# An attention and feed-forward kernel: one batch instead of two ahead of the matrix products, three first tiles in four passes of four chunks

## The chip, the cores and the metric

The kernel runs on one core of a Trainium2 chip. The metric is the device time of one execution in microseconds (us). Three runs of the kernel before took 1062.29, 1059.40 and 1056.72 us, median 1059.4. The execution that was profiled took 1056.42 us by the same clock; its span from the first to the last instruction is 1054.7 us.

The engines are named as in the profile: PE (TensorE, matrix products), PEld (its weight loads), DVE (VectorE), ACT (ScalarE), POOL (GpSimd) and SP (SyncE, which here only issues DMAs).

## The reference

Eight batches, eight heads, 576 positions, 64 numbers per head; then a feed-forward layer over all 4608 tokens with 512 inputs, 2048 inner features and `g = h cos h` between the products.

```python
q_d, k_d, v_d = (a.reshape(B, H, 144, 4, D).mean(axis=3) for a in (q, k, v))
out_d  = softmax(q_d @ k_d.T / 8) @ v_d              # 144 x 144 per head
out_up = np.repeat(out_d, 4, axis=2)
scores = np.where(abs(i - j) < 4, q @ k.T / 8, -1e9)  # a band of 7 keys per query
x = (out_up + softmax(scores) @ v)                   # 576 x 64 per head
x = x.transpose(0, 2, 1, 3).reshape(4608, 512)
h = x @ w_in                                         # w_in 512 x 2048, float64
out = (h * cos(h)) @ w_out                           # w_out 2048 x 512, float64
```

## The kernel before

**Tiles and steps.** The 4608 tokens are cut into 12 tiles of 384 (`NT`), the 2048 features into 16 chunks of 128 (`NC`). A *step* is one chunk of one tile: `gemm1` (L673) makes 12 matmuls (L685) for `h`, ACT and DVE work out `h cos h` (L696 to L704), and two steps later (`LAG`) `gemm2` (L709) adds the chunk's 9 matmuls (L721) into three PSUM banks `po.0` to `po.2`. So a step has 21 matmuls, and there are 192 steps. Both products use a high and a low part of each number (`x0h`, `x0l`, `gh`, `gl`, `wi`, `wo`), which `sub` (L384) makes on POOL or DVE. `PASSES` (L36) is the order of the steps: tiles 0, 1, 2 with chunks 0 to 3, then tiles 0, 1, 2 with chunks 4 to 15, then tiles 3 to 11 with all 16. At the end of a pass the three banks are copied out by ACT (L737) and stored; the first pass of a tile stores through SP (L743), a later pass adds to what is in memory through a DMA that POOL issues (L746). Steps are counted from 0 in this document: tile 1 begins at step 4, chunk 4 is first used at step 12, tile 3 begins at step 48.

**Attention.** A *unit* is one batch and one pair of heads: 32 units of 219 matmuls. `u_qk` (L456) loads q and k and sums groups of four; `u_v` (L481) loads v twice and sums groups of four, on POOL by two additions (L490, L491) or on DVE by one reduction (L492); `u_s` (L496) makes the scores (L513, L521) and the softmax (L534 to L583); `u_t` (L586) transposes (L595, L606); `u_pv` (L612) multiplies by v (L623, L634), adds both parts (L642) and writes the high and low parts of x (L657 to L659). Tile 0 needs batch 0, tile 1 needs batches 0 and 1, tile 2 needs batch 1, tile 3 needs batch 2. x has four slots (`NX`), so tile 4 is written where tile 0 was read. Batches 0 and 1 (`NEARLY`) run ahead of the first step, with PSUM banks that the matrix products use later (`bank`, L444) and with buffers cut from the places of weight chunks 6 to 15 (`ub`, L433). In these early units the row maximum is scaled by a DVE instruction of its own (L557), the exponentials are taken on ACT straight from PSUM (L564), and the last scaling runs on POOL or DVE (L582). Later batches share three banks `pa.0` to `pa.2`.

**Weights.** Weights arrive as float64 words. `w_load` (L389) loads 512 KB; `w_split` (L399) turns it into a high and a low part by an ACT copy (L407), four DVE instructions (L408, L410, L412, L414), an ACT or DVE copy (L418) and a subtraction on POOL or DVE (L386). There are 32 such splits, two per chunk. Their staging buffer is the high half of x slot 3 (L345, L405), and x slot 3 is not written before the last split is through (L364).

**Order.** Nothing runs in the order of the text. `Plan` (L78) collects the operations with their dependencies, costs and due times (`at`, L752), and a list scheduler (L164, L255) lays them out on the engines; each engine then works through its list in that order. Where an operation has alternatives (`alts`), the scheduler picks the engine that would end it earlier. Due times of attention units and weights are given in steps (L759 to L791); those of batch 2 lie between the last step of tile 0, which frees the x slot that tile 4 takes, and the first step of tile 3; `BOOST` (L51) raises the priority of units of batches 0 and 1. All early loads go through one SP queue in the order of `chain` (L804): q and k of batch 0, v of batch 0, q and k of batch 1, weights of chunk 0, v of batch 1, then the other weights. Where PE has a gap in the plan before 300 us, it is filled with matmuls of 128 columns on an identity (L835).

Of the kernel before, what the change touches and what calls it, by code (L numbers as in the profile page):

```python
# [17 lines left out]
ALU = mybir.AluOpType  # L18
# [16 lines left out]
NF = 4  # L35
PASSES = [(t, 0, NF) for t in range(3)] + [(t, NF, NC) for t in range(3)] + [(t, 0, NC) for t in range(3, NT)]  # L36
SD = S // 4
# [12 lines left out]
ON_PE = ()  # L50
BOOST = {0: 100.0, 1: 60.0}  # L51
LAG = 2
# [246 lines left out]
def attn_ffn_kernel(ctx: ExitStack, tc: tile.TileContext, qT, kT, vdn, vl, w_in, w_out, out):  # L299
# [144 lines left out]
    def bank(b, kind):  # L444

        if b < NEARLY:
            tags = {"s": ("pa.0", "po.0", "pa.1", "po.1"), "t": ("ph.0", "ph.1"), "v": ("pa.2", "po.2")}[kind]
            return psum(tags[int(pl.turn("early" + kind, len(tags))[-1])])
        return psum(pl.turn("pa", 3))
# [31 lines left out]
    def u_v(b, pr):  # L481
# [6 lines left out]

        def v_pool():
            pool.tensor_tensor(out=v4()[:, :, 0:2, :], in0=v4()[:, :, 0:2, :], in1=v4()[:, :, 2:4, :], op=ALU.add)  # L490
            pool.tensor_tensor(out=vd.get(), in0=v4()[:, :, 0, :], in1=v4()[:, :, 1, :], op=ALU.add)  # L491
        pl.op("POOL", 2.2, v_pool, w=[vd, vd4], alts=[("DVE", 1.93, lambda: dve.tensor_reduce(  # L492
            out=vd.get(), in_=v4().rearrange("p a r n -> p a n r"), axis=AX.X, op=ALU.add))])
        st[(b, pr)].update(vd=vd, vl=vt)

    def u_s(b, pr):  # L496
# [58 lines left out]
        if early:  # L555

            pl.op("DVE", 0.08, lambda: dve.tensor_scalar(out=mxd.get(), in0=mxd.get(), scalar1=1.0 / 128.0, scalar2=None, op0=ALU.mult),  # L557
                  w=[mxd])

            def exps():  # L560
                act.activation(sml.get(), sml.get(), AF.Exp, scale=0.125)
                for h in range(2):
                    for i in range(2):
                        act.activation(smd.get()[:, h, i], dq(h)[:, i], AF.Exp, bias=mxd.get()[:, h, i:i + 1], scale=1.0 / 128.0,  # L564
                                       accum_out=sud()[:, h, i:i + 1])
            o = pl.op("ACT", _act(n, False) + 4 * (_act(SD, True, 2) + 0.1), exps, r=[mxd, su] + poo, w=[sml, smd], pw=[su2], tab="exp")
            for bk in banks:
# [13 lines left out]
        for sm, part, size, bc in ((sml, sul, n, bl), (smd, sud, m, bd)):  # L581
            f = lambda e, sm=sm, part=part, bc=bc: lambda: e.tensor_tensor(out=sm.get(), in0=sm.get(), in1=bc(part()), op=ALU.mult)  # L582
            pl.op("POOL", _pool(size), f(pool), r=[su], w=[sm], alts=[("DVE", _dve(size), f(dve))])  # L583
        u["sml"], u["smd"] = sml, smd
# [185 lines left out]
    for c in range(NC):  # L770
        for k, d in (("i", 0.0), ("o", 0.7)):
            t = need[c] if c < NF else NF + c - NF
            at(t + d - 4.0, w_load, k, c)
# [3 lines left out]
    for i in range(NPAIR):  # L777
        for t, f in ((-7.9 + 0.5 * i, u_qk), (-4.4 + 0.5 * i, u_v), (-3.4 + i, u_s), (-2.4 + i, u_t), (-1.4 + i, u_pv)):
            at(t, f, 1, i)
# [21 lines left out]
    def ul(f, b):  # L801
        return [(f, b, i) for i in range(NPAIR)]

    chain = [o for k in ul("u_qk", 0) + ul("u_v", 0) + ul("u_qk", 1) + wl(0) + ul("u_v", 1) + wl(*range(1, NC))  # L804
             for o in loads[k]]
    for o, n in zip(chain, chain[1:]):
# [21 lines left out]
    with tc.manual_schedule():  # L828
        constants()
        for o in order:  # L830
            if o.eng == "PE" and o.start < CFG["fend"]:
                s = spare(last, o.start)
                n = int((o.start - s[0] - CFG["fgap"]) / (0.107 if last < 5 else 0.058)) if s else 0
                for _ in range(n):
                    pe.matmul(s[2].get()[:, 0:P], ident_b, ident_b, start=True, stop=True)  # L835
                last = o.start + o.dur
# [36 lines left out]
```

## Time and profile before

| what | value |
|---|---|
| median of three runs | 1059.4 us |
| the profiled execution: time, span | 1056.42 us, 1054.7 us |
| mean granted TensorE clock | 0.974 of full |
| PE busy | 1019.1 us (97%), 11447 matmuls |
| DVE busy | 664.5 us (63%) |
| ACT busy | 619.1 us (59%) |
| POOL busy | 195.8 us (19%) |
| first matmul of step 0 | 87.38 us |

PE is busy nearly all the time after the first fifth, but a busy PE may be a filler or run at half clock, so the share alone tells little of the beginning. The windows below give each engine's busy time per stretch, the number of matmuls in brackets, the granted clock (PEclk, 1.00 is 2.4 GHz and 0.50 is 1.2 GHz) and the share of time in which the 16 DMA engines were busy.

### The profile page before, as it was taken

The page shows a single profiled execution, that of the slowest core. Times are in us where ns is not written, and L with a number is a line of the kernel's source. Part 1 is how long each engine was busy: PE and PEld are TensorE (multiplying, and loading weights), DVE is VectorE, ACT ScalarE, POOL GpSimd, SP SyncE. Part 2 cuts the span into 40 slices and gives each one's busy share as a digit, 9 for nine tenths or more (in the row PEclk, how much of TensorE's full clock was granted, in tenths as well). Part 3 has the DMA queues.
Part 4 walks back from the last instruction along what each step waited for, and adds up shares of the span by engine and source line. Part 5 has one row for each costly group of instructions (what it writes and reads, how often), then busy time and mean ns, then how long its engine had stood idle before and what let it go on. Part 6 is the DMA issues. An engine that isn't in the chain of part 4 may idle for free.

```text
span 1054.7 us, 26617 instructions
## 1 busy us (share of the span) xinstructions
PE 1019.1 (97%) x11447; PEld 899.3 (85%) x11447; DVE 664.5 (63%) x1315; ACT 619.1 (59%) x1194; POOL 195.8 (19%) x239
## 2 busy tenths in 40 slices
PE   6888987999999999999999999999999999999998
PEld 5767876988888898888898888888888888999997
DVE  6686999976548755654636865746546864544442
ACT  2344677766566756655656665646656665655554
POOL 5633445331112310201001310201010300000000
PEclk9577999999999999999999999999999999999999
DMA  9295061031122500300101420301100410000000
GB/s 305 80 346 212 21 215 46 1 55 26 50 57 74 126 31 25 107 24 27 54 27 46 122 63 23 103 18 38 54 27 24 130 54 1 31 1 1 30 1 31
DMA packets 33862, 71.45 MB, mean 68 GB/s; under 512 B 3152, under 2 KB 11344, under 8 KB 33744
## 3 DMA queue, kind: packets, MB, share of 16 engines
q1 hardware_dynamic: 32448, 67.38, 20.0%
q0 software_dynamic: 1296, 2.36, 1.6%
q8 instruction: 90, 1.47, 0.6%
q14 instruction: 28, 0.23, 0.1%
HBM read 57.93 MB, written 11.80 MB: 66 GB/s over the span
## 4 chain that ended last, share of the span: by engine, by line
PE 86%; DVE 8%; issue 3%; ACT 1%; ACTq 0%; POOL 0%; POOLq 0%; DVEq 0%
PE bank L721 34%; PE bank L685 34%; PE bank L634 5%; PE bank L513 3%; PE bank L835 2%; PE bank L623 2%; PE bank L521 2%; DVE xxh L412 2%; PE bank L606 2%; DVE xxh L414 1%; DVE xxh L408 1%; PE bank L595 1%; DVE tr L697 1%; DVE xxh L410 1%; DVE tr L700 1%
## 5 line engine op out<-in xcount | busy, mean ns | idle before, releaser
L721 PE MATMUL bank<-wo,gh 128*128 128x512 f32 x1152 | 365.0, 398 | 0.1
L721 PEld LDWEIGHTS bank<-wo,gh 128*128 128x128 f32 x1152 | 208.8, 188 | 37.4 <-issue 4.0
L721 PE MATMUL bank<-wo,gl 128*128 128x512 f32 x576 | 228.2, 396 | 0.6 <-DVE gl L386 0.5
L700 DVE SCALAR_TENSOR_TENSOR tr<-tr,bank 128x384 f32<-128x384 f32 x192 | 105.8, 551 | 144.1 <-ACT tr L695 144.1
L696 ACT ACTIVATE tr<-bank,bmagic 128x384 f32<-128x384 f32 x192 | 111.3, 580 | 120.2 <-PE bank L685 115.3
L697 DVE SCALAR_TENSOR_TENSOR tr<-tr,bank 128x384 f32<-128x384 f32 x192 | 105.7, 550 | 101.9 <-ACT tr L696 101.5
L694 ACT ACTIVATE tr<-tr 128x384 f32<-128x384 f32 x192 | 100.7, 525 | 84.8 <-DVE tr L697 84.4
L702 ACT ACTIVATE gh<-tr 128x384 fp32r<-128x384 f32 x173 | 90.6, 524 | 95.9 <-DVE tr L700 95.0
L386 DVE TENSOR_TENSOR gl<-tr,gh 128x384 fp32r<-128x384 f32 x163 | 92.9, 570 | 73.2 <-ACT gh L702 72.1
L721 PEld LDWEIGHTS bank<-wo,gl 128*128 128x128 f32 x576 | 108.0, 187 | 25.7 <-DVE gl L386 1.3
L685 PE MATMUL bank<-x0h,wi 128*128 128x384 f32 x384 | 108.6, 344 | 5.7 <-DVE tr L700 5.4
L685 PE MATMUL bank<-x2h,wi 128*128 128x384 f32 x384 | 106.9, 339 | 2.3 <-DVE tr L700 2.3
L685 PE MATMUL bank<-x1h,wi 128*128 128x384 f32 x384 | 106.8, 339 | 1.0 <-DVE tr L700 1.0
L685 PE MATMUL bank<-x3h,wi 128*128 128x384 f32 x384 | 106.9, 339 | 0.1
L695 ACT ACTIVATE tr<-tr 128x384 f32<-128x384 f32 x192 | 100.8, 525 | 6.1
L386 POOL TENSOR_TENSOR gl<-tr,gh 128x384 fp32r<-128x384 f32 x29 | 32.5, 1122 | 313.7 <-DVE gh L703 250.3
L685 PEld LDWEIGHTS bank<-x0h,wi 128*128 128x128 f32 x384 | 71.1, 190 | 9.8 <-DVE tr L700 7.2
L685 PEld LDWEIGHTS bank<-x2h,wi 128*128 128x128 f32 x384 | 70.2, 188 | 5.1 <-DVE tr L700 2.4
L685 PEld LDWEIGHTS bank<-x1h,wi 128*128 128x128 f32 x384 | 70.2, 188 | 4.4 <-DVE tr L700 2.1
L685 PEld LDWEIGHTS bank<-x3h,wi 128*128 128x128 f32 x384 | 70.2, 188 | 2.7 <-issue 0.6
L685 PE MATMUL bank<-x0l,wi 128*128 128x384 f32 x192 | 65.2, 340 | 0.0
L685 PE MATMUL bank<-x3l,wi 128*128 128x384 f32 x192 | 64.5, 336 | 0.0
(188 smaller groups left out, 1501.0 us busy)
## 6 DMA issues: line engine op xcount, KB each, us to landing
vl<-vl SPq DMA_DIRECT2D x26, 384.0 KB
out<-ob SPq DMA_DIRECT2D x36, 256.0 KB
wdi<-w_in SPq DMA_DIRECT2D x16, 512.0 KB
wdo<-w_out SPq DMA_DIRECT2D x16, 512.0 KB
q<-qT SPq DMA_DIRECT2D x26, 292.0 KB
k<-kT SPq DMA_DIRECT2D x26, 292.0 KB
vd<-vdn SPq DMA_DIRECT2D x26, 288.0 KB
out<-ob POOLq DMA_DIRECT2D x9, 256.0 KB, 6.2
```

The source lines that it names most:

```text
L386: f = lambda e: lambda: e.tensor_tensor(out=out(), in0=in0(), in1=in1(), op=ALU.subtract)
L412: pl.op("DVE", 0.7, lambda: dve.scalar_tensor_tensor(out=vi(), in0=wd()[:, :, 1], scalar=-0x40000000, in1=vi(), op0=ALU.bitwise_and, op1=A ...
L513: pe.matmul(banks[h].get()[BS * i:BS * (i + 1), LQ + BS * s:LQ + BS * (s + 1)], q.get()[hs, o:o + BS], k.get()[hs, o:o + BS], start=True, ...
L634: pe.matmul(banks[e].get()[64 * h:64 * h + 64, o:o + BQ], vt.get()[r, a, i, :], ptl.get()[r, a, i, :], start=True, stop=True)
L685: pe.matmul(ph.get()[:, :m], w[:, i, kc, :], x[:, kc, :], start=(n == 0), stop=(n == 3 * KC - 1))
L694: act.activation(tr.get(), tr.get(), AF.Sin, scale=PI)
L695: act.activation(tr.get(), tr.get(), AF.Square)
L696: pl.op("ACT", _act(m, True, 1), lambda: act.activation(tr.get(), h(), AF.Identity, bias=bmagic), r=[ph], w=[tr])
L697: pl.op("DVE", _dve(m), lambda: dve.scalar_tensor_tensor(out=tr.get(), in0=tr.get(), scalar=MAGIC, in1=h(), op0=ALU.subtract, op1=ALU.subt ...
L700: pl.op("DVE", _dve(m), lambda: dve.scalar_tensor_tensor(out=tr.get(), in0=tr.get(), scalar=0.5, in1=h(), op0=ALU.subtract, op1=ALU.mult), ...
L702: pl.op("ACT", _act(m, False), lambda: act.activation(gh.get(), tr.get(), AF.Copy), r=[tr], w=[gh], alts=[("DVE", _dve(m / 2), lambda: dve ...
L721: pe.matmul(o, (gh, gh, gl)[k].get()[:, sl], wo.get()[:, (0, 1, 0)[k]], start=(c == c0 and k == 0), stop=(c == c1 - 1 and k == 2))
```

## The change

- Batch 0 alone keeps the early banks; batch 1 uses the three banks `pa.0` to `pa.2` in turn, has due times from step -4 to step 3.7 instead of -7.9 to 1.6, and half of its former boost (30 for 60).
- `PASSES`: tiles 0, 1, 2 take chunks 0 to 3, then 4 to 7, then 8 to 11, then 12 to 15. Weights of a chunk are due at the step that first uses it: chunks 4 to 7 at step 12, 8 to 11 at step 24, 12 to 15 at step 36 (before, chunk c at step c).
- By the same rule the last step of tile 0 becomes 39 (before 23), so the units of batch 2 are due from step 37.5 to 44.5 instead of 21.5 to 44.5.
- The order of early loads: q and k of batch 0, v of its pairs 0 and 1, weights 0, v of its pairs 2 and 3, weights 1, q and k of batch 1, weights 2, v of batch 1, then the other weights.
- The sum of v may run as two additions on either POOL or DVE; the reduction is gone.
- In early units the scaling of the row maximum moves from DVE into the ACT block, and the last scaling of the 144 x 144 part may also run on ACT, in four instructions.
- Fillers have 512 columns instead of 128, and a quarter of the number per gap.

```diff
-PASSES = [(t, 0, NF) for t in range(3)] + [(t, NF, NC) for t in range(3)] + [(t, 0, NC) for t in range(3, NT)]
+PASSES = [(t, c, c + NF) for c in range(0, NC, NF) for t in range(3)] + [(t, 0, NC) for t in range(3, NT)]
-BOOST = {0: 100.0, 1: 60.0}
+BOOST = {0: 100.0, 1: 30.0}
     def bank(b, kind):
-        if b < NEARLY:
+        if b == 0:
     def u_v(b, pr):
-        def v_pool():
-            pool.tensor_tensor(out=v4()[:, :, 0:2, :], in0=v4()[:, :, 0:2, :], in1=v4()[:, :, 2:4, :], op=ALU.add)
-            pool.tensor_tensor(out=vd.get(), in0=v4()[:, :, 0, :], in1=v4()[:, :, 1, :], op=ALU.add)
-        pl.op("POOL", 2.2, v_pool, w=[vd, vd4], alts=[("DVE", 1.93, lambda: dve.tensor_reduce(
-            out=vd.get(), in_=v4().rearrange("p a r n -> p a n r"), axis=AX.X, op=ALU.add))])
+        def v_add(e):
+            def f():
+                e.tensor_tensor(out=v4()[:, :, 0:2, :], in0=v4()[:, :, 0:2, :], in1=v4()[:, :, 2:4, :], op=ALU.add)
+                e.tensor_tensor(out=vd.get(), in0=v4()[:, :, 0, :], in1=v4()[:, :, 1, :], op=ALU.add)
+            return f
+        pl.op("POOL", 2.2, v_add(pool), w=[vd, vd4], alts=[("DVE", 1.1, v_add(dve))])
     def u_s(b, pr):
-            pl.op("DVE", 0.08, lambda: dve.tensor_scalar(out=mxd.get(), in0=mxd.get(), scalar1=1.0 / 128.0, scalar2=None, op0=ALU.mult),
-                  w=[mxd])
             def exps():
+                act.activation(mxd.get(), mxd.get(), AF.Copy, scale=1.0 / 128.0)
                 act.activation(sml.get(), sml.get(), AF.Exp, scale=0.125)
...
+            if early and sm is smd:
+                def scaled():
+                    for h in range(2):
+                        for i in range(2):
+                            act.activation(smd.get()[:, h, i], smd.get()[:, h, i], AF.Copy, scale=sud()[:, h, i:i + 1])
+                alts.append(("ACT", 4 * _act(SD, False, 1), scaled))
...
-            t = need[c] if c < NF else NF + c - NF
+            t = need[c]
...
-        for t, f in ((-7.9 + 0.5 * i, u_qk), (-4.4 + 0.5 * i, u_v), (-3.4 + i, u_s), (-2.4 + i, u_t), (-1.4 + i, u_pv)):
+        for t, f in ((-4.0 + 0.5 * i, u_qk), (-2.4 + 0.5 * i, u_v), (-0.9 + i, u_s), (-0.1 + i, u_t), (0.7 + i, u_pv)):
...
-    chain = [o for k in ul("u_qk", 0) + ul("u_v", 0) + ul("u_qk", 1) + wl(0) + ul("u_v", 1) + wl(*range(1, NC))
-             for o in loads[k]]
+    chain = [o for k in ul("u_qk", 0) + ul("u_v", 0)[:2] + wl(0) + ul("u_v", 0)[2:] + wl(1) + ul("u_qk", 1) + wl(2) + ul("u_v", 1)
+             + wl(*range(3, NC)) for o in loads[k]]
...
-                n = int((o.start - s[0] - CFG["fgap"]) / (0.107 if last < 5 else 0.058)) if s else 0
+                n = int((o.start - s[0] - CFG["fgap"]) / (0.43 if last < 5 else 0.23)) if s else 0
-                    pe.matmul(s[2].get()[:, 0:P], ident_b, ident_b, start=True, stop=True)
+                    pe.matmul(s[2].get(), ident_b, ident_b.unsqueeze(1).broadcast_to([P, 4, P]), start=True, stop=True)
```

## Rows read from the trace of the kernel before

**Rows 1.** Busy time by stretch: busy us (instructions) per engine, PEclk, DMA share, GB/s.

```profile
0.00:50.00 50.00, 37.70 (x1065) 32.03 (x1066) 31.51 (x72) 14.13 (x50) 30.04 (x60) 0.76 0.62 202
...
120.70:222.00 101.30, 91.75 (x538) 79.03 (x537) 100.72 (x166) 74.58 (x141) 44.91 (x38) 0.98 0.23 75
222.00:341.10 119.10, 119.07 (x1289) 105.27 (x1288) 73.03 (x150) 73.03 (x134) 20.88 (x26) 1.00 0.23 52
341.10:429.60 88.50, 87.72 (x1213) 76.53 (x1213) 60.30 (x122) 55.13 (x103) 17.43 (x22) 1.00 0.26 65
920.00:1040.00 120.00, 120.00 (x605) 108.87 (x604) 48.80 (x88) 63.31 (x118) 0.00 (x0) 1.00 0.04 14
```

**Rows 2.** The two stretches between 50 us and step 4, same columns.

```profile
50.00:87.40 37.40, 33.05 (x797) 28.56 (x796) 27.70 (x68) 16.88 (x59) 12.77 (x13) 0.72 0.80 276
87.40:120.70 33.30, 29.42 (x449) 26.86 (x447) 28.66 (x49) 19.70 (x38) 14.14 (x15) 0.90 0.43 148
```

**Rows 3.** Timeline of PE (start us, us, line): first matmuls of steps 4 and 48.

```profile
120.68 0.33 PE L685 MATMUL bank<-x1h,wi 128*128 128x384 f32 x1
...
341.13 0.45 PE L685 MATMUL bank<-x3h,wi 128*128 128x384 f32 x1
```

**Rows 4.** DVE by line, 0 to 120.7 us: count | busy us, mean ns | idle before.

```profile
L408 DVE TENSOR_SCALAR xxh<-xxh 128x512 f32<-128x512 f32 x10 | 5.4, 542 | 3.6 <-ACT xxh L407 3.6
L410 DVE TENSOR_SCALAR xxh<-xxh 128x512 int32<-128x512 int32 x10 | 5.3, 530 | 0.0
L414 DVE SCALAR_TENSOR_TENSOR xxh<-wdi,xxh 128x512 int32<-128x512 int32 x5 | 4.3, 865 | 0.0
L412 DVE SCALAR_TENSOR_TENSOR xxh<-wdo,xxh 128x512 int32<-128x512 int32 x4 | 4.2, 1051 | 0.0
L557 DVE TENSOR_SCALAR mxd<-mxd 72x4 f32<-72x4 f32 x8 | 4.1, 516 | 0.0
L414 DVE SCALAR_TENSOR_TENSOR xxh<-wdo,xxh 128x512 int32<-128x512 int32 x4 | 3.7, 932 | 0.0
...
L412 DVE SCALAR_TENSOR_TENSOR xxh<-wdi,xxh 128x512 int32<-128x512 int32 x5 | 3.4, 679 | 0.0
...
L386 DVE TENSOR_TENSOR wo<-xxh,wo 128x512 fp32r<-128x512 f32 x4 | 3.1, 774 | 0.1
L492 DVE TENSOR_REDUCE wxo<-wxi 72x256 f32<-72x1024 f32 x1 | 1.9, 1941 | 0.0
```

**Rows 5.** Timeline of PE: an early stop, and four first products of units with v.

```profile
12.01 0.28 PE L513 MATMUL bank<-wxo,wxi 64*32 64x32 f32 x12 [4.22 <-issue]
...
72.77 0.43 PE L634 MATMUL bank<-ptl,vl 32*64 32x24 f32 x16
...
89.90 0.48 PE L634 MATMUL bank<-wxi,wxo 32*64 32x24 f32 x20
...
335.90 1.30 PE L634 MATMUL bank<-ptl,vl 32*64 32x24 f32 x76
...
381.18 1.53 PE L634 MATMUL bank<-ptl,vl 32*64 32x24 f32 x91
```

**Rows 6.** Timeline of ACT: x of batch 0's third pair, and the first weight split.

```profile
51.28 0.35 ACT L657 ACTIVATE x1h<-wxo 128x192 fp32r<-128x192 f32 x1
51.53 0.66 ACT L407 ACTIVATE xxh<-wdi 128x512 f32<-128x512 f32 x1
```

**Rows 7.** Lines L737 and L746: ns min/median/max, first and last start; who waited.

```profile
L737 ACT ACTIVATE ob<-bank x36: 577/598/620, 130.8 to 1050.1; 128x512 f32<-128x512 f32 x36
...
  PEld bank L721: 0.6, 2
...
L746 POOL DMA_DIRECT2D out<-ob x9: 873/1170/1549, 230.2 to 356.6; - x9
```

**Rows 8.** Timeline of POOL and of DVE, 15 to 18 us.

```profile
15.67 1.90 POOL L490 TENSOR_TENSOR wxi<-wxi 72x512 f32<-72x512 f32 x1 [3.15 <-DMA wxi<-vdn]
...
16.36 1.24 DVE L557 TENSOR_SCALAR mxd<-mxd 72x4 f32<-72x4 f32 x1
```

More of the change, by code (lines that the diff above doesn't have):

```diff
@@ L565, in exps @@
                                        accum_out=sud()[:, h, i:i + 1])
-            o = pl.op("ACT", _act(n, False) + 4 * (_act(SD, True, 2) + 0.1), exps, r=[mxd, su] + poo, w=[sml, smd], pw=[su2], tab="exp")
+            o = pl.op("ACT", _act(n, False) + 4 * (_act(SD, True, 2) + 0.1) + 0.15, exps, r=[su] + poo, w=[mxd, sml, smd], pw=[su2], tab="exp")
             for bk in banks:
@@ L582, in u_s @@
             f = lambda e, sm=sm, part=part, bc=bc: lambda: e.tensor_tensor(out=sm.get(), in0=sm.get(), in1=bc(part()), op=ALU.mult)
-            pl.op("POOL", _pool(size), f(pool), r=[su], w=[sm], alts=[("DVE", _dve(size), f(dve))])
+            alts = [("DVE", _dve(size), f(dve))]
+            if early and sm is smd:
[4 more added lines that the diff above has]
+                alts.append(("ACT", 4 * _act(SD, False, 1), scaled))
+            pl.op("POOL", _pool(size), f(pool), r=[su], w=[sm], alts=alts)
         u["sml"], u["smd"] = sml, smd
```

## The prediction

> **What bounds the kernel now.** I read the windows first, then the timeline of PE for the starts of steps, then the lines of DVE in the beginning. From 341 us on there is nothing to win: PE is busy 87.72 of 88.5 us and all of 120.0 us in the late window [rows 1]. That late window holds 605 matmuls, 605 / 21 = 28.8 steps, so a step costs 120 / 28.8 = 4.165 us. The window from 341.1 to 429.6 us holds 16 steps and four units (1213 = 336 + 4 x 219 matmuls and one more), so a unit costs (88.5 - 16 x 4.165) / 4 = 5.46 us of PE. The window before it, from 222.0 to 341.1 us, has 1289 matmuls, that is 24 steps and 3.58 units: 100.0 + 19.5 = 119.5 us of work in 119.1 us. So PE is full there too, and whatever the kernel loses it has lost by 222 us.
>
> How much: by then 24 steps (100.0 us) and 8.42 units (46.0 us) are done, and 222 - 146 = 76 us are lost. Step 4, the first that needs batch 1, begins at 120.68 us [rows 3] with 4 steps (16.7) and 8 units (43.7) done: 60 of the 76 us are lost before it. The other 16 fall between 120.7 and 222 us, where 20 steps and 0.42 units (85.6 us) take 101.3 us.
>
> What held PE up is DVE: from 120.7 to 222 us it is busy 100.72 of 101.3 us [rows 1]. Before step 4 it is the nearest to full of the helpers without being full: 31.51 us in the first 50, then 27.70 of 37.4 and 28.66 of 33.3 us [rows 1, 2], together 87.9 of 120.7 and so 32.8 us idle. The weight splits are what fills it: their seven groups up to step 4 sum to 5.4 + 5.3 + 4.3 + 4.2 + 3.7 + 3.4 + 3.1 = 29.4 us for 9 to 10 splits [rows 4], some 3.1 us each. The order counts as well: three of batch 0's four pairs have their x by 51.6 us, and the first split begins only then [rows 6], since its words were loaded behind all of batch 0 and the q and k of batch 1.
>
> **The change part by part.** I work out when step 4, step 36 and step 48 begin.
>
> *Up to step 4.* The work of both batches must be done as before. DVE loses: the eight scalings of the maximum, 4.1 us [rows 4]; two reductions of 1.9 us against two pairs of additions. These I put at 0.7 + 0.4 us (the 128x512 subtraction of 0.774 us [rows 4], and half of it), so 2 x 0.8 = 1.6 us less. If the scheduler moves two more sums from POOL to DVE, as their lower cost invites, 2.2 us come back, and the net is between +0.6 and -1.6; I take 0. The largest part are splits: step 4 needs six (four of w_in, two of w_out, since gemm2 lags by two steps) where DVE had made 9 to 10, so 29.4 - 6 x 3.1 = 10.8 us move behind step 4. DVE then has 87.9 - 4.1 - 10.8 = 73 us to do. Its idle time I keep nearly whole: 18.5 of the 32.8 us fall into the first 50 us, where loads, PE's own stops (one of 4.22 us with no wait shown [rows 5]) and chains of short instructions make it, which the change leaves; of the other 14.3 us I give back two. Step 4 at 73 + 30 = 103 us.
>
> The scaling on ACT is hidden: ACT is busy 50.7 of 120.7 us [rows 1, 2], and eight small copies at no more than the 0.35 us of a 192-column copy [rows 6] are 2.8 us. If a copy stood on the chain of a unit it would cost what the DVE instruction did (mean 0.516 us), so from -4 to +3 us over both batches. The option to scale the 144 x 144 part on ACT is four copies of at most 0.35 us against 0.7 us of DVE: I count 0 (between -5 and +3).
>
> The bounds of step 4: below, DVE's idle time of the first 50 us alone, 73 + 18.5 = 91 us. Above, the three banks: a unit of batch 1 now waits for the banks of the one before it. On nine banks four units followed each other in (89.90 - 72.77) / 3 = 5.7 us; later batches on three banks, with PE full, took (381.18 - 335.90) / 3 = 15.1 us [rows 5]. Batch 0's last x at some 53 us, the first unit of batch 1 multiplied by v at 60, three more at 15.1 and 5 us for sums and casts: 110 us; with two such waits more, 121, no earlier than before.
>
> Weights 0 move ahead of the v of pairs 2 and 3: 1 MB, so those come later by some 4 us at the 202 GB/s of the first stretch to 5 us. They are used after 30 us and land before, so 0 (0 to 5). Splits can then begin in the gaps of batch 0, so step 0 follows batch 0 directly; its four steps (16.7 us) run in the time of batch 1, beside its 21.8 us of PE work: 38.5 us in 50.
>
> *Steps 4 to 36.* PE has 32 x 4.165 = 133.3 us. DVE has 32 x 1.69 us of step work (48.80 us in the 28.8 late steps) = 54, and 26 splits. From 120.7 to 222 us the 100.7 us of DVE held 33.9 us of steps, 3.5 us of a unit (a unit takes (60.30 - 16 x 1.69) / 4 = 8.3) and 22.5 splits, so 2.8 us each; 26 are 73 us. Together 127 against 133.3 us: PE bounds, DVE is 95% full, and the two will not mesh wholly. I add 4 us (0 to 12, the upper end from the 16 us lost with DVE full).
>
> Six more ends of passes: 18 copies of 0.598 us on ACT (10.8 us; it is busy 74.58 of 101.3) and 18 accumulating DMAs of 1.17 us on POOL (21 us; busy 44.91 of 101.3, and 20.88 of the next 119). Behind such a DMA stand POOL's subtractions, whose results gemm2 reads two steps later, which covers them. The two waits of PE's loads for such copies were 0.6 us together [rows 7]; six give 1.8 us, and I add 2 (0 to 6). Step 36 at 103 + 133.3 + 6 = 242 us.
>
> *Steps 36 to 48.* All of batch 2 falls here: 12 steps and four units, 50.0 + 21.8 = 71.8 us, and I add 2. Step 48 at 316 us against 341.1 [rows 3], with the same work done. After it nothing changes. 25 us less of 1056.4 (the profiled execution; span 1054.7 and 1.7 around it) is 1031.4; that execution is 3 us under the median of 1059.4, so I forecast **1033 us**.
>
> The wider fillers cost 0: a quarter of the number, four times the length; PE is not the bound where they stand (1 us either way).
>
> One rule of the Trainium skill weighs against the additions on DVE. A DVE instruction on four columns that begins inside a POOL addition takes 1.24 us [rows 8], where its eight average 0.516 us [rows 4]. The Trainium skill, "SBUF — State Buffer", section "SBUF: two separate sides", says that a DVE instruction with two SBUF inputs and a POOL instruction that reads SBUF hold a shared port pair exclusively, the second waiting for all of the first. The additions have two such inputs; by that rule four of them would each wait up to 1.9 us for a POOL addition, and the forecast would be up to 7 us later, 1040.
>
> **The rivals.**
>
> *Nothing gained at step 4.* Order is the scheduler's, and the chain of batch 1 on three banks may fill the time. For it: 15.1 us per unit on three banks; the 0.72 to 0.76 of granted clock in the first 87 us, at whose lower level (1.2 GHz) the 38.5 us between steps 0 and 4 would be 77. Against it: 15.1 us was seen with PE full of steps, and from 87.4 us the clock was at 0.90. Step 4 at 118 to 121 us leaves 5 us of the gain: 1051 to 1058.
>
> *The squeeze at batch 2, slower than before.* The last splits are now due at step 36 to 39, x slot 3 can't be written before they end, and the slot that tile 4 takes is free only after step 39. Batch 2's products with v therefore start at some 267 us (two steps' slack past 242 + 16.7) and are done at 267 + 3c + 5 with c the time from unit to unit; PE's own work ends at 316. At c = 15.1 that is 317: no stall. The point from which it decides is c = 25, where the stall eats the 25 us; at c = 28 tile 3 waits 40 us and the time is 1072. For it: four units in 8 steps, with DVE at 95% before. Against it: the units of [rows 5] are never so far apart.
>
> *More than forecast.* DVE's idle time before step 4 falls to 18.5 us and steps 4 to 36 mesh: step 48 at 91 + 133 + 72 = 296 to 302, the time 1012 to 1019.
>
> **How the numbers follow.** Forecast, 1020 to 1045: 0.62. A smaller gain of the same kind, 1045 to 1054: 0.10. Nothing gained: 0.11. Squeeze: 0.08. More: 0.09. A change of 0.5%, 5.3 us, is about what can be told from none here. Faster by over 0.5%: 0.62 + 0.10 + 0.09 = 0.81; within it 0.11; slower 0.08. The range leaves out the squeeze and half of "more": 1015 to 1056.
>
> **What would show it.** Step 0 within 45 to 60 us; step 4 near 103; the reduction and the DVE scaling gone; splits spread to some 235 us; DVE under 97% between steps 4 and 36; step 36 near 242, step 48 near 316, and the same distance from there to the end. It is wrong if step 4 begins after 115 us, if PE idles over 12 us between steps 4 and 36, or if tile 3 waits for x over 5 us.

## The result and the profile after

The changed kernel takes 1046.69 us (median of four runs, 1045.35 to 1047.73) against 1060.03 us for the kernel before beside it. The ratio is 0.9876 with a 95% interval of 0.9847 to 0.9905: 13.3 us faster, 10 to 16 by the interval. Forecast were 1033 us, 26 less. The direction was right, the size about half. The profiled execution took 1046.31 us, span 1044.5 us, 10.1 us less than the one of before.

First the starts of steps 0, 4 and 48, in the timeline of PE after (start us, us, line), to be set against [rows 3]:

```profile
59.71 0.52 PE L691 MATMUL bank<-x0h,wi 128*128 128x384 f32 x1
...
114.68 0.69 PE L691 MATMUL bank<-x1h,wi 128*128 128x384 f32 x1
...
331.65 0.52 PE L691 MATMUL bank<-x3h,wi 128*128 128x384 f32 x1
```

| us | before | forecast | after |
|---|---|---|---|
| step 0 begins | 87.4 | 45 to 60 | 59.7 |
| step 4 | 120.7 | 103 | 114.7 |
| step 36 | | 242 | 260.4 |
| step 48 | 341.1 | 316 | 331.6 |
| steps 4 to 36 take | | 139.3 | 145.7 |
| steps 36 to 48 take | | 73.8 | 71.3 |
| step 48 to the end of the span | 713.6 | 713.6 | 712.9 |

Step 48 is 15.6 us later than forecast: 11.7 of it are there at step 4, 6.4 come in steps 4 to 36, and 2.5 are given back in steps 36 to 48. Nothing is lost or won after it. The windows of after, cut at the steps (columns as in [rows 1]):

```profile
0.00:59.70 59.70, 51.58 (x1042) 34.17 (x1043) 41.04 (x94) 21.10 (x76) 24.26 (x50) 0.71 0.78 246
59.70:114.70 55.00, 48.48 (x990) 35.09 (x988) 52.69 (x106) 32.25 (x83) 24.14 (x23) 0.91 0.58 202
...
114.70:210.00 95.30, 90.07 (x436) 77.57 (x434) 89.04 (x154) 69.07 (x129) 43.38 (x34) 0.98 0.31 84
210.00:260.40 50.40, 50.36 (x253) 45.65 (x254) 30.08 (x55) 32.25 (x64) 10.08 (x11) 1.00 0.34 48
114.70:260.40 145.70, 140.43 (x689) 123.23 (x688) 119.12 (x208) 101.32 (x192) 53.46 (x45) 0.99 0.32 72
...
260.40:331.60 71.20, 71.20 (x1124) 60.75 (x1123) 54.12 (x114) 46.31 (x85) 21.09 (x24) 1.00 0.49 108
```

Two things are to be read in the third busy column, DVE's. Before step 4 it holds 41.04 + 52.69 = 93.7 us where the forecast had 73, and between steps 0 and 4 DVE is full, 52.69 of 55.00 us. And steps 4 to 36 are not even: in the first 95.3 us (20 steps) DVE is 93% busy and PE loses 5.2 us; in the next 50.4 us (12 steps) DVE is 60% busy and PE loses nothing. The splits fill the first part: of 32, 11 begin before step 4 and 30 before step 24, the last at 217 us. Before, the last began at 219 us. Chunks 12 to 15 are first used at 260 us. So the splits did not move to where they are needed. What PE waits for in those 95.3 us (us in total, times, longest):

```profile
PE bank L691 <- DVE tr L706: 3.1, 4, 1.0
PE bank L727 <- POOL gl L386: 0.8, 1, 0.8
PE bank L727 <- DVE ob L744: 0.6, 2, 0.4
```

L706 is the DVE instruction that ends the use of `gemm1`'s bank; it stands behind split instructions, of which DVE has these in the same stretch:

```profile
L408 DVE TENSOR_SCALAR xxh<-xxh 128x512 f32<-128x512 f32 x19 | 14.8, 777 | 0.0
...
L412 DVE SCALAR_TENSOR_TENSOR xxh<-wdi,xxh 128x512 int32<-128x512 int32 x10 | 10.2, 1023 | 0.0
L410 DVE TENSOR_SCALAR xxh<-xxh 128x512 int32<-128x512 int32 x18 | 10.2, 572 | 0.0
```

On the side of step 4 the scores of batch 1's four units (L514; min/median/max ns, then first and last start) show how its chain runs over three banks. The four begin at 48.8, 63.8, 76.0 and 90.8 us, 14.0 us apart; the 33 instructions of the first row beyond 96 are a part of those of batch 2.

```profile
L514 PE MATMUL bank<-k,q x129: 208/238/260, 48.8 to 112.0; 64*32 64x32 f32 x129
L514 PE MATMUL bank<-xxl x96: 186/193/214, 63.8 to 64.9; 64*32 64x32 f32 x96
L514 PE MATMUL bank<-wxi,wxo x96: 187/193/213, 76.0 to 77.1; 64*32 64x32 f32 x96
L514 PE MATMUL bank<-wxo,wxo x96: 186/193/213, 90.8 to 91.6; 64*32 64x32 f32 x96
```

The chain ends with batch 1's last part of x, which POOL writes (before, then after):

```profile
107.64 0.78 POOL L386 TENSOR_TENSOR x1l<-wxi,x1h 128x192 fp32r<-128x192 f32 x1
```

```profile
112.02 0.59 POOL L386 TENSOR_TENSOR x1l<-wxi,x1h 128x192 fp32r<-128x192 f32 x1 [4.21 <-ACT x1h L663]
```

Before, batch 1 was complete at 108.4 us, and step 4 came 12.3 us later, behind steps 0 to 3, which began only at 87.4. Now step 4 follows batch 1 by 2.1 us, but batch 1 is complete 4.2 us later, at 112.6. So the change took away the 12.3 us behind batch 1, and batch 1 itself became slower.

Step 0 waits too, for its weights. The x of batch 0 is complete at 52.9 us (first line), the low part of the first weights only at 60.7 (second line). From 51.5 us to step 0 PE runs fillers, and inside step 0 it waits for that low part (third line):

```profile
52.31 0.55 DVE L386 TENSOR_TENSOR x0l<-wxi,x0h 128x384 fp32r<-128x384 f32 x1
...
57.84 2.90 POOL L386 TENSOR_TENSOR wi<-xxh,wi 128x512 fp32r<-128x512 f32 x1 [7.08 <-ACT wi L418]
...
60.80 0.62 PE L691 MATMUL bank<-x0h,wi 128*128 128x384 f32 x2 [0.40 <-POOL wi L386]
```

### The profile page after: what moved, and what is told of

It is laid out like the page before. It is cut to its first block, busy times and chain, and to the rows that moved or that the text cites. A ratio compares the mean times of both kernels' runs of the same rounds, so it can differ in the third digit from the quotient of the medians.

```text
span 1044.5 us, 26106 instructions
## 1 busy us (share of the span) xinstructions
PE 1019.7 (98%) x11157; PEld 880.8 (84%) x11157; DVE 680.8 (65%) x1355; ACT 620.7 (59%) x1209; POOL 179.9 (17%) x220
## 4 chain that ended last, share of the span: by engine, by line
PE 79%; DVE 2%; issue 1%; ACT 1%; POOL 0%; ACTq 0%; DVEq 0%
PE bank L727 35%; PE bank L691 34%; PE bank L640 4%; PE bank L514 2%; PE bank L629 1%; PE bank L522 1%; PE bank L612 1%; PE bank L601 1%; DVE xxh L412 1%; DVE tr L703 0%; DVE gl L386 0%; DVE xxh L408 0%; POOL gl L386 0%; DVE xxh L414 0%; DVE tr L706 0%
## 5 line engine op out<-in xcount | busy, mean ns | idle before, releaser
L706 DVE SCALAR_TENSOR_TENSOR tr<-tr,bank 128x384 f32<-128x384 f32 x192 | 105.8, 551 | 134.4 <-ACT tr L701 133.8
L700 ACT ACTIVATE tr<-tr 128x384 f32<-128x384 f32 x192 | 100.8, 525 | 81.7 <-DVE tr L703 81.4
L386 DVE TENSOR_TENSOR gl<-tr,gh 128x384 fp32r<-128x384 f32 x157 | 90.8, 578 | 70.7 <-ACT gh L708 69.0
L691 PE MATMUL bank<-x2h,wi 128*128 128x384 f32 x384 | 107.0, 339 | 1.0 <-DVE tr L706 1.0
L386 POOL TENSOR_TENSOR gl<-tr,gh 128x384 fp32r<-128x384 f32 x35 | 43.1, 1232 | 311.5 <-DVE gh L709 217.4
L691 PEld LDWEIGHTS bank<-x1h,wi 128*128 128x128 f32 x384 | 71.3, 191 | 3.9 <-DVE tr L706 1.3
L691 PE MATMUL bank<-x1l,wi 128*128 128x384 f32 x192 | 65.2, 340 | 0.0
L691 PE MATMUL bank<-x2l,wi 128*128 128x384 f32 x192 | 64.5, 336 | 0.0
```

What stands on the lines that cost most here:

```text
L386: f = lambda e: lambda: e.tensor_tensor(out=out(), in0=in0(), in1=in1(), op=ALU.subtract)
L691: pe.matmul(ph.get()[:, :m], w[:, i, kc, :], x[:, kc, :], start=(n == 0), stop=(n == 3 * KC - 1))
L700: act.activation(tr.get(), tr.get(), AF.Sin, scale=PI)
L706: pl.op("DVE", _dve(m), lambda: dve.scalar_tensor_tensor(out=tr.get(), in0=tr.get(), scalar=0.5, in1=h(), op0=ALU.subtract, op1=ALU.mult), ...
```

## The experiments

Each kernel is the changed one with the edit shown (e9: the kernel before), and was timed in three rounds beside the kernel before, whose median was between 1057.6 and 1060.0 us in the different groups of runs; across groups the ratios are the better measure. "4 to 36" is the time from the first matmul of step 4 to that of step 36 in the profiled execution; the executions of a kernel (four, in e9 seven) lie up to 8.5 us apart (e13, whose profile is of its fastest, 1030.3 us), so one profile is read with that in mind.

| run | median us | ratio to before (95%) | step 0 | step 4 | 4 to 36 | step 48 |
|---|---|---|---|---|---|---|
| after | 1046.7 | 0.9876 (0.9847, 0.9905) | 59.7 | 114.7 | 145.7 | 331.6 |
| e1 late splits | 1038.6 | 0.9796 (0.9759, 0.9833) | 55.6 | 113.7 | 137.2 | 323.0 |
| e2 early banks | 1036.9 | 0.9779 (0.9742, 0.9815) | 82.6 | 110.2 | 141.6 | 323.8 |
| e3 sums on POOL | 1048.3 | 0.9887 (0.9857, 0.9917) | 63.8 | 123.3 | 139.5 | 335.0 |
| e4 two passes | 1047.3 | 0.9878 (0.9848, 0.9909) | 55.0 | 118.1 | other work | 334.5 |
| e5 = e1 + e2 | 1028.9 | 0.9726 (0.9711, 0.9740) | 84.6 | 107.0 | 134.0 | 315.2 |
| e6 constant 0.171 | 1038.2 | 0.9821 (0.9791, 0.9851) | 56.8 | 111.8 | 140.7 | 323.2 |
| e7 more fillers | 1048.2 | 0.9911 (0.9896, 0.9926) | 62.6 | 116.7 | 144.8 | 332.8 |
| e8 loads of before | 1039.5 | 0.9832 (0.9811, 0.9854) | 61.3 | 104.6 | 147.8 | 322.8 |
| e9 before, 0.185 | 1050.4 | 0.9921 (0.9895, 0.9946) | 85.7 | 117.4 | other work | 333.9 |
| e10 after, 0.185 | 1047.0 | 0.9894 (0.9857, 0.9931) | 52.1 | 114.2 | 144.7 | 333.9 |
| e11 e1, 0.185 | 1041.1 | 0.9834 (0.9799, 0.9868) | 65.9 | 115.0 | 139.2 | 326.7 |
| e12 e5, 0.185 | 1043.0 | 0.9856 (0.9817, 0.9894) | 87.4 | 111.9 | 135.1 | 327.4 |
| e13 = e1 + e8 | 1035.7 | 0.9788 (0.9760, 0.9817) | 61.2 | 103.5 | 139.6 | 315.2 |
| e14 e13, 0.185 | 1038.9 | 0.9816 (0.9783, 0.9850) | 61.9 | 110.6 | 139.4 | 324.7 |
| e15 q, k earlier | 1038.1 | 0.9802 (0.9780, 0.9824) | 65.9 | 114.5 | 136.8 | 322.4 |
| e16 = e5 + e8 | 1040.3 | 0.9824 (0.9804, 0.9844) | 91.6 | 111.7 | 138.9 | 323.9 |
| e17 splits narrow | 1032.9 | 0.9764 (0.9740, 0.9788) | 57.5 | 107.8 | 137.5 | 316.7 |
| e18 later splits narrow | 1039.1 | 0.9817 (0.9796, 0.9838) | 60.2 | 116.3 | 136.5 | 324.1 |

**The splits, e1.** The theory: they begin long before they are needed and take DVE from the steps. The rival: DVE's step work and the four passes cost this by themselves. The edit makes the planner place the first instruction of a split of chunks 4 to 15 behind a step shortly before its use (`pe1` holds `gemm1`'s PE operations).

```diff
+        j = 2 * (c % NF) + (k == "o")
+        gate = {0: None, 1: 4 + j, 2: 12 + 1.5 * j, 3: 24 + 1.5 * j}[c // NF]
         pl.op("ACT", _act(n, False), lambda: act.activation(v.get(), ..., AF.Abs), r=[wd_b], w=[v],
+              after=[] if gate is None else [pe1[int(gate)]])
```

> The changed kernel with one thing more: the weight splits of chunks 4 to 15 are held back in the written order until a step shortly before they are needed (one per step from step 4, then two per three steps), so none of them stands before step 4. Theory A (VectorE's work sets step 4, and it does work there that could wait; the changed kernel has 11 splits begun by step 4 where 8 belong to chunks 0 to 3): 3 splits of 2.7 us less, step 4 at about 107 us instead of 114.7; splits end near 250 us instead of 220; PE loses under 4 us between steps 4 and 36 instead of 12; time 1034 to 1038. Theory B (the chain of batch 1 over three banks, 12 us from unit to unit, sets step 4): step 4 stays within 3 us of 114.7, only the loss after it shrinks, time 1038 to 1043.

Eight splits now begin before step 4, and the last at 245 us. Steps 4 to 36 fall from 145.7 to 137.2 us, the time to 1038.6. DVE's windows for 4 to 24 and 24 to 36 (third busy column) are now 92% and 85%, and PE is full in both:

```profile
113.70:200.60 86.90, 86.76 (x421) 78.10 (x421) 80.16 (x149) 65.12 (x123) 23.98 (x22) 0.97 0.35 96
200.60:250.80 50.20, 50.20 (x253) 45.52 (x252) 42.68 (x82) 36.07 (x68) 9.23 (x10) 1.00 0.33 48
```

Step 4, with three splits fewer in front of it, moved by 1.0 us only, as theory B had it.

**Batch 1 on the early banks again, e2.**

```diff
-BOOST = {0: 100.0, 1: 30.0}
+BOOST = {0: 100.0, 1: 60.0}
-        if b == 0:
+        if b < NEARLY:
```

and batch 1's due times of before.

> The changed kernel with batch 1 put back on the early banks, with its due times and boost of before; passes, load order, sums and fillers as changed. Theory A (VectorE's work): step 4 within 4 us of 114.7, as VectorE has the same to do; time 1043 to 1049. Theory B (three banks): units of batch 1 follow each other in 6 us as before instead of 12, step 4 at 95 to 103 us, time 1030 to 1037. What speaks against B in the outcome: step 0 may come later, since batch 1 then goes ahead of it.

The scores of batch 1 begin 5.9 us apart here, (68.6 - 51.0) / 3, against 14.0:

```profile
L514 PE MATMUL bank<-k,q x192: 186/193/259, 51.0 to 90.2; 64*32 64x32 f32 x192
L514 PE MATMUL bank<-xxl x96: 207/238/258, 57.5 to 58.5; 64*32 64x32 f32 x96
L514 PE MATMUL bank<-wxi,wxo x96: 186/193/213, 64.6 to 65.4; 64*32 64x32 f32 x96
L514 PE MATMUL bank<-wxo,wxo x96: 187/193/213, 68.6 to 69.4; 64*32 64x32 f32 x96
```

Step 0 comes behind products of the units, at 82.6 us, and yet step 4 begins at 110.2, no later than in after: just outside theory A's 4 us and far from theory B's 95 to 103, though the time lies in B's range. Overlapping steps 0 to 3 with batch 1, which is what the change is made of, gains nothing at step 4 against this order. Since the edit changes banks, due times and boost together, and no steps stand between the units here, the pace of 5.9 us is not that of the banks alone.

**The sums of v on POOL alone, e3**, without the DVE alternative:

```diff
-        pl.op("POOL", 2.2, v_add(pool), w=[vd, vd4], alts=[("DVE", 1.1, v_add(dve))])
+        pl.op("POOL", 2.2, v_add(pool), w=[vd, vd4])
```

> The changed kernel with all sums of v on GpSimd (no alternative). VectorE did 6 of the early 8 in 8.5 us. Theory A: step 4 earlier by 4 to 8 us, time 1039 to 1043. Theory B: GpSimd's 2 us per sum are beside the chain, step 4 within 3 us, time 1044 to 1049.

In after six of the eight early sums had moved to DVE, 8.5 us in all against 3.8 before. Taking them away did not relieve DVE in this order: it is busy 94.4 us before step 4 (93.7 in after). One split more begins before step 4, and six copies out of PSUM (2.4 us) came over from ACT. POOL's busy time there rises from 48.4 to 66.3 us, and the first instruction of a split takes longer: the row of after (11 splits before step 4), then that of e3 (12).

```profile
L408 DVE TENSOR_SCALAR xxh<-xxh 128x512 f32<-128x512 f32 x11 | 4.9, 463 | 0.0
```

```profile
L408 DVE TENSOR_SCALAR xxh<-xxh 128x512 f32<-128x512 f32 x12 | 7.8, 659 | 1.9 <-ACT xxh L407 1.9
```

Step 4 came at 123.3, later than either theory had it. The Trainium skill, "SBUF — State Buffer", section "SBUF: two separate sides", has DVE and POOL share a port pair which one holds while the other waits; these rows agree with it in direction.

**Two passes as before, e4** (`PASSES` and the weights' due times of before, all else changed):

```diff
-PASSES = [(t, c, c + NF) for c in range(0, NC, NF) for t in range(3)] + [(t, 0, NC) for t in range(3, NT)]
+PASSES = [(t, 0, NF) for t in range(3)] + [(t, NF, NC) for t in range(3)] + [(t, 0, NC) for t in range(3, NT)]
-            t = need[c]
+            t = need[c] if c < NF else NF + c - NF
```

> The changed kernel with the two passes of before (chunks 0 to 3, then 4 to 15) and their due times. If the four passes are worth what the prediction said (splits spread over steps 4 to 36, some 6 to 10 us less PE idle): 1052 to 1057. If they are worth nothing because the splits run ahead anyway (they end at 220 us in both kernels): 1044 to 1049, step 4 within 3 us of 114.7.

1047.3 against 1046.7 us: no gain of the four passes is to be seen in these two orders. The splits run ahead with either list of passes (the last begins at 212 us here, at 217 in after), which is the likely reason; by e6 an order can hide a difference of this size.

**Both, e5** (the edits of e1 and e2).

> Late splits and the early banks for batch 1 together. If the two shortfalls are separate (late splits took 8.6 us out of steps 4 to 36 and left step 4 at 113.7; the banks brought step 4 to 110.2 and left steps 4 to 36 at 141.6): step 4 at 108 to 111, 135 to 138 us from there to step 36, time 1026 to 1031. If both are one and the same cause (VectorE's work before step 24): no better than either, 1035 to 1039.

1028.9 us, the fastest kernel of the study and 2.7% under the kernel before (ratio 0.9711 to 0.9740). But see e12.

**How much an order is worth, e6.** The planner's constant `late` from 0.17 to 0.171 changes nothing in the work and draws another order.

```diff
-... latpe=0.25, late=0.17,
+... latpe=0.25, late=0.171,
```

> The changed kernel with nothing changed but one latency of the planner's costs, 0.171 for 0.170: the same work in an order that comes out otherwise. It measures how far a time may move by the order alone. Theory A and B both: within 3 us of 1046.7; if it moves by more than 5 us, ablations under that size tell nothing.

1038.2 against 1046.7 us: 8.5 us for an edit without meaning, as much as e1 or e2 gave (by the ratios 0.9821 against 0.9876, some 6 us, with intervals that just touch; step 48 lies 8.4 us earlier in the profiles). From here on a difference of total times is trusted only if it returns in another order or if the written order is the same.

**The clock, e7.** From 26.3 to 53.6 us the granted clock is at its lower level in after. Twelve more fillers of 512 columns behind batch 0's first unit raise it; the order of all other instructions stays.

```diff
                 n = int((o.start - s[0] - CFG["fgap"]) / (0.43 if last < 5 else 0.23)) if s else 0
+                if o.name == "u_pv" and o.arg == (0, 0) and o.dur < 1.0 and s:
+                    n = max(n, 12)
```

> The changed kernel with the same written order and 12 more wide fillers on TensorE ahead of the first dense product with v of batch 0, right behind the stop of 2.23 us at 24.1 us after which the clock was at half from 26.3 to 53.6 us with TensorE busy 26.6 of 27 us. Theory C (half clock over batch 0 is what makes step 0 and with it step 4 late): the clock is at full from some 31 us, batch 0's x is complete 4 to 7 us earlier, step 0 at 54 to 57 instead of 59.7 us, step 4 3 to 6 us earlier, time 1040 to 1044. Theories A and B: the 4 us of fillers are lost or hidden, step 4 within 2 us, time 1045 to 1050.

The window of after, then that of e7 (PEclk is the number behind the five busy columns):

```profile
33.20:43.40 10.20, 10.20 (x219) 8.51 (x217) 7.17 (x15) 4.63 (x15) 2.80 (x5) 0.50 0.55 167
```

```profile
33.20:43.40 10.20, 9.18 (x246) 6.63 (x244) 7.48 (x18) 6.88 (x23) 2.64 (x4) 1.00 0.56 177
```

Ten us at full clock, and step 0 at 62.6, step 4 at 116.7, both later. By 43.4 us PE has run 474 + 99 + 219 = 792 matmuls in after and 474 + 82 + 246 = 802 in e7 (windows to 26.3, 33.2 and 43.4 us), 12 of them the added fillers: the same work. The half clock in this stretch is not what holds the beginning up. No run raises the clock in the other stretches, such as the last 10 us before step 4 (PEclk 0.91 between steps 0 and 4 of after).

**The load order of before, e8.**

```diff
-    chain = [o for k in ul("u_qk", 0) + ul("u_v", 0)[:2] + wl(0) + ul("u_v", 0)[2:] + wl(1) + ul("u_qk", 1) + wl(2) + ul("u_v", 1)
-             + wl(*range(3, NC)) for o in loads[k]]
+    chain = [o for k in ul("u_qk", 0) + ul("u_v", 0) + ul("u_qk", 1) + wl(0) + ul("u_v", 1) + wl(*range(1, NC))
+             for o in loads[k]]
```

> The changed kernel with the order of early loads of before (all of batch 0 and q, k of batch 1 ahead of the first weights). If loading weights 0 early is what lets step 0 follow batch 0: step 0 at 70 us or later, step 4 at 117 to 122, time 1048 to 1054. If step 4 is set by batch 1's chain alone: step 0 later by under 10 us, step 4 within 3 us, time 1044 to 1049.

Batch 1's first scores begin at 34.8 instead of 48.8 us, those of its last unit at 81.7 instead of 90.8, and step 4 at 104.6. Neither theory had that: step 0 came at 61.3, not at 70 or later, and step 4 moved by 10.1 us, not by under 3. Undoing this one part of the change brings step 4 within 2 us of the 103 forecast.

**Other orders, e9 to e12.** `late=0.185` for 0.17, on the kernel before (e9), on after (e10), on e1 (e11) and on e5 (e12).

> The kernel before with one latency of the planner's costs at 0.185 for 0.170, and nothing else: the spread that the written order alone gives to the kernel before. Order theory: anything from 1049 to 1068, 3 to 9 us off. If the order of before is no lottery: within 3 us of 1058.

> The changed kernel with the same edit of 0.185 for 0.170. Order theory (the first redraw gave 1038.2 for 1046.7, so the changed kernel's own order is a poor draw): 1034 to 1044, from step 4 to step 36 139 to 148 us as in all orders with free splits. If the first redraw was the lucky one: 1044 to 1050.

> Late splits (as e1) with 0.185 for 0.170. If holding the splits back is what fills TensorE after step 4, whatever the order: from step 4 to step 36 133 to 138 us, as in e1 and e5, against 139 to 148 in all orders without it; time 1030 to 1040 depending on step 4. If e1 was a draw: 139 us or more.

> Late splits and the early banks for batch 1 (as e5) with 0.185 for 0.170. If e5's gain is of its two parts: step 4 at 105 to 111, 133 to 138 us from there to step 36, time 1026 to 1033. If it was a good draw: 1035 or more.

The kernel before falls to 1050.4 by another order, so with 0.185 the whole change is worth 1050.4 - 1047.0 = 3.4 us by medians, and the two ratios' intervals overlap. e10's 1047.0 lies in the range of its second theory: of the changed kernel's three orders, that of e6 is the lucky one. e11's 139.2 us for steps 4 to 36 is more than the 133 to 138 expected of late splits, and just in the range given to a draw; it is 5.6 us less than its pair e10. e5's 1028.9 becomes 1043.0: its lead was in part a lucky order.

**Late splits and loads, e13 to e16.** e13 has the edits of e1 and e8, e14 the same with 0.185, e15 that of e1 and only q and k of batch 1 ahead of weights 1, e16 the edits of e5 and e8.

```diff
e15:
-    ... wl(0) + ul("u_v", 0)[2:] + wl(1) + ul("u_qk", 1) + wl(2) + ...
+    ... wl(0) + ul("u_v", 0)[2:] + ul("u_qk", 1) + wl(1) + wl(2) + ...
```

> Splits of chunks 4 to 15 held back as in e1, and the load order of the kernel before (q and k of batch 1 ahead of all weights). If the arrival of q and k of batch 1 sets where its chain over three banks starts: first scores of batch 1 near 35 us, step 4 at 104 to 107 us. If the three banks' pace alone sets step 4: 112 to 115 us. Steps 4 to 36 take 134 to 139 us by the theory of the splits (143 us without it). Time by both theories 1026 to 1032 us; by the splits alone 1036 to 1041 us.

> The same edit with the planner's constant late at 0.185, which only draws another order. If the two causes add up whatever the order: step 4 at 104 to 107 us, steps 4 to 36 134 to 139 us, time within 5 us of e13. If e13's gain is a lucky order: step 4 at 112 us or later.

> Splits held back, and of the load order only this: q and k of batch 1 ahead of the weights of chunk 1 rather than behind them; the weights of chunk 0 stay where the change put them. If the arrival of q and k sets the chain's start: first scores of batch 1 some 4 to 8 us earlier than the 47 us of e1, and step 4 as much earlier than e1's 113.7 us, 106 to 110 us. If not: 113 to 115 us.

> Splits held back, load order of before, and batch 1 on the early banks as in e2 and e5. If with the early banks the load order no longer decides (its chain is short): step 4 near e5's 107 us and time 1027 to 1032 us. If the load order gives its 7 us here too: step 4 near 100 us and time 1021 to 1026 us. If the order drawn outweighs both: above 1036 us.

The scores of batch 1 begin at 30.9 (e13), 36.6 (e14), 44.8 (e15) and 36.4 us (e16). Against the kernels with late splits in the same constant (e1: 47.2, e11: 50.2) step 4 follows in e13 (103.5, 10.2 us earlier) and partly in e14 (110.6, 4.4 earlier), not in e15 and e16; in e15 the edit moved the start by 2.4 us only, less than expected. e13's time, 1035.7, missed the 1026 to 1032 that both theories together gave. In e14 the units stand 17.1 us apart, (88.0 - 36.6) / 3: an early start is lost again on the way. With three banks the load order of before is faster in all three pairs, by 7.2 (after, e8), 2.9 (e1, e13) and 2.1 us (e11, e14); the ratios' intervals overlap in all three, in the first only just.

**The same written order with less DVE work, e17 and e18.** The four DVE instructions of a split work on 32 of 512 columns, for all chunks (e17) or for chunks 4 to 15 (e18). The rest of each weight tile is left unsplit, so these two kernels do not compute the reference. The planner's costs are left as they were, so every engine keeps the order of after.

```diff
-        wd, n = wd_b.get, DM
+        wd, n, z = wd_b.get, DM, slice(0, 32)                         # e17
+        wd, n, z = wd_b.get, DM, slice(0, 32 if c >= NF else DM)      # e18
-        pl.op("DVE", 0.5, lambda: dve.tensor_scalar(out=v.get(), in0=v.get(), ...
+        pl.op("DVE", 0.5, lambda: dve.tensor_scalar(out=v.get()[:, z], in0=v.get()[:, z], ...
```

> The four DVE instructions of every split work on 32 of 512 columns (so the weights are wrong); all engines keep the written order of the changed kernel. Before step 4 eleven splits have 0.49 + 0.47 + 0.67 + 0.89 = 2.5 us of DVE each there; at some 0.6 us on 32 columns DVE's work before step 4 falls by about 21 us, from 93.7 to the 73 us of the prediction. If DVE's work sets step 4: 103 us or earlier. If the chain of batch 1 over three banks sets it: 110 to 115 us, with the scores of its units still some 14 us apart. Steps 4 to 36: 134 to 137 us if only DVE held them up.

> The same, but only for chunks 4 to 15: the eight splits that steps 0 to 3 need stay whole, the three begun too early are cut, and so is everything of the splits between steps 4 and 36 on DVE. Written order as in the changed kernel. By the theory that splits begun too early hold up steps 4 to 36 through DVE: 134 to 137 us there instead of 145.7, time about 10 us less. If something else than DVE's load does it: 143 us or more. Step 4: 114 if the chain of batch 1 sets it, some 109 if DVE's work does (three splits at 1.9 us less).

e18, steps 4 to 36 in one window (third busy column: DVE), against the window 114.70:260.40 of after with as many matmuls:

```profile
116.30:252.80 136.50, 136.50 (x688) 123.40 (x687) 82.29 (x206) 100.79 (x192) 43.92 (x45) 0.99 0.33 77
```

DVE has 82.3 us to do instead of 119.1, PE idles 0 instead of 5.3 us, and the stretch is 9.2 us shorter. The other 3.9 us of that are longer busy time of PE (140.43 against 136.50), which no run takes apart. Same order, same matmuls: DVE's load by splits is shown as the cause there. Step 4 itself, with three splits cut in front of it, came no earlier (116.3). e17 up to step 4, in the two stretches before and after step 0:

```profile
0.00:57.50 57.50, 50.41 (x1043) 34.59 (x1043) 38.65 (x94) 21.57 (x77) 25.35 (x51) 0.73 0.79 251
57.50:107.80 50.30, 44.95 (x990) 33.11 (x988) 41.63 (x107) 31.56 (x83) 18.16 (x22) 0.97 0.63 220
```

and the scores of batch 1:

```profile
L514 PE MATMUL bank<-k,q x192: 186/238/260, 47.3 to 106.4; 64*32 64x32 f32 x192
L514 PE MATMUL bank<-xxl x96: 186/193/214, 60.9 to 62.0; 64*32 64x32 f32 x96
L514 PE MATMUL bank<-wxi,wxo x96: 186/193/214, 71.6 to 72.8; 64*32 64x32 f32 x96
L514 PE MATMUL bank<-wxo,wxo x96: 186/193/213, 86.2 to 87.0; 64*32 64x32 f32 x96
```

DVE's work before step 4 is 38.65 + 41.63 = 80.3 us, 13.4 less than in after (I had expected 21; the groups of narrow instructions still take 0.17 to 0.44 us on average). Step 4 moved by 6.9 us, half of that, to 107.8, between the two theories, and the units still begin 13.0 us apart, (86.2 - 47.3) / 3. DVE idles 27.5 of 107.8 us, but 18.9 of these lie before step 0; from step 0 to step 4 it is still 83% busy. So of step 4's 11.7 us over the forecast 6.9 go with the 13.4 us of DVE work that is gone here. The clock may have part in that: PEclk between steps 0 and 4 is 0.97 here and 0.91 in after. The other 4.8 us stay with a DVE that still has 7.3 us more to do than the forecast's 73. That step 48 then begins at 316.7, near the forecast's 316, is chance, since this kernel has less split work than the forecast counted on.

## Why the prediction was half right

- **"10.8 us [of splits] move behind step 4" failed.** I took the due times for the order. 11 splits began before step 4 where I had counted six, and 10 before: in this scheduler a due time ranks what is ready, it does not hold anything back (and it ranks in the first of eight trial runs only; the later ones go by a run from the end), and words and DVE were there early.
- **"The net [of the sums] is between +0.6 and -1.6" failed too.** I let two sums move from POOL to DVE; four did (two were there before, six now), 8.5 us against 3.8, and an addition of 512 columns took 0.95 us instead of 0.7 (5.7 us in six). With the 10.8 us these are the largest parts of the 93.7 us of DVE that I had put at 73.
- **The order of loads had no price at step 4.** I priced weights 0 ahead of batch 0's v, and put nothing down for weights 0 and 1 ahead of the q and k of batch 1. With the order of before its first scores begin 14.0, 16.3 and 13.6 us earlier, and step 4 10.1, 10.2 and 4.4 us earlier (e8, e13, e14).
- **"Step 0 follows batch 0 directly" failed.** Its 59.7 us lie in the 45 to 60 stated, but 6.9 us behind batch 0's x: the first split ended late.
- **"Step 4 at 73 + 30 = 103" failed as a form of sum as well.** A sum over DVE has no chain in it; with the 93.7 us measured it would give 124, since DVE idled 21.0 us, not 30. I had the chain of batch 1 on three banks at 15.1 us per unit from [rows 5] and set it aside because those rows had PE full; it measured 14.0, and 13.0 with DVE relieved. In all 14 kernels with three banks for batch 1 step 4 begins 21 to 26 us after the first scores of its last unit. It was the rival "nothing gained at step 4", with its mechanism, though 3 to 6 us earlier than its 118 to 121; the time fell into "a smaller gain of the same kind", which I gave 0.10. In five orders of the three-bank kernel with the new load order (after, e1, e6, e10, e11) step 4 lies between 111.8 and 115.0, with other work in e3 and e4 at 123.3 and 118.1.
- **"Splits spread to some 235 us" failed, and with it "I add 4 us" for steps 4 to 36.** They took 145.7 instead of 139.3. With splits held back they took 134.0 to 139.6 us in eight kernels (e1, e5, e11 to e16), without 139.5 to 147.8 in seven (after, e2, e3, e6, e7, e8, e10): the two ranges meet, and the pairs tell more. The four that differ in that edit alone (after and e1, e2 and e5, e8 and e13, e10 and e11) are 8.5, 7.6, 8.3 and 5.6 us apart, and their medians 8.1, 8.0, 3.8 and 6.0 (the ratios' intervals are apart in the first two). The forecast's 139.3 fits kernels that do what I had assumed.
- **Right:** DVE's split work as what fills the beginning (e18 for steps 4 to 36, e17 in part for step 4); the added ends of passes small (PE waited 0.8 us for `ob` and its weight loads 2.0 us in steps 4 to 24); steps 36 to 48 at 71.3 us with PE full, so no squeeze at batch 2; nothing changed after step 48. That the scalings on ACT cost nothing no run tests.
- **The signs of being wrong were set too wide.** Step 4 at 114.7 stayed under the 115, and PE idled 5.3 us between steps 4 and 36, under the 12. Yet that stretch is 12.4 us longer than its 133.3 us of work, so idle time alone shows less than half of the loss.
- **Three sums are off, by little.** The times of DVE's instructions up to step 4 of before add up to 100.7 us where it is busy 87.9, since they overlap; so 10.8 us of them taken off the busy time is some tenth too much. 1031.4 and 3 us make 1034, not 1033; and a stall that eats 25 us needs c = 23 by the squeeze's own formula, not 25; neither bears on the result.
- **The rule of the Trainium skill**, "SBUF — State Buffer", section "SBUF: two separate sides", gave 1040 in the prediction, nearer than 1033, but by luck: the six additions of 512 columns took 0.68 to 1.32 us, together 1.7 us more than six of the quickest, where the bound by the rule was 7 for four. In e3 some of the work taken off DVE and put on POOL came back as longer DVE instructions. It was not the main part.

What the change itself is worth stays uncertain by the order: 13.3 us with the constant 0.17, 3.4 with 0.185. Two things are open. Why step 4 stays at 107.8 with little split work is not settled between the chain's pace, its late start, the clock and DVE's other work: the load order moves the start by 2 to 16 us, but its effect at step 4 was 10, 10, 4 and -1 us (e8, e13, e14, e15). Nor is it shown whether three banks, or the steps between the units, set the pace. And the early banks gave 9.8 and 9.7 us with the constant 0.17 (e2, e5), cost 1.9 with 0.185 (e12 against e11) and 4.6 with the other loads (e16 against e13).

## What to carry to other kernels

A later due time moves work only if something holds it back: look at when the first and last of it run, and add a dependency where they must wait. Where a chain of units shares few buffers, multiply its measured pace by the units and put it beside the engine's sum; the later of the two is the safer estimate (here 110 us rather than 103; 114.7 came). Ask what each load is put behind in its queue, and not only what is put ahead. Where a scheduler writes the order, redraw it once with an edit that means nothing before an ablation of the same size is read, and test a suspected load by making its instructions smaller in the same written order.

## What the runs showed that I had not expected

An order drawn anew moved the kernel before by 8.9 us (e9, 0.9921 of it, 0.9895 to 0.9946), the changed one by 8.5 us (e6) or by 0.3 (e10), and the fastest kernel by 14.1 us (e5 and e12): up to as much as each part of the change. Raising the clock for 10 us in the beginning bought nothing (e7). And one DVE instruction of 128x512, the first of a split, has no single price. In after, in steps 4 to 24 (min/median/max ns, first and last start):

```profile
L408 DVE TENSOR_SCALAR xxh<-xxh x19: 409/416/1523, 122.7 to 208.5; 128x512 f32<-128x512 f32 x19
```

The 8 of them during which no POOL instruction ran average 415 ns, the 11 that meet one 1039 ns (four of these took 409 to 418 all the same). So a split beside POOL's work costs DVE more than one at rest: the two after 210 us, with POOL still, took 418 ns on average.
